# Attention followed by a gated feed-forward layer on one core: four of the twelve f chunks of the first two batches go through the pair scheme, and their weights are loaded later

## The chip, the cores and the metric

The kernel runs on one core of one Trainium2 chip. The metric is the device time of one execution in microseconds (us), as the median of several runs. TensorE is called PE below, VectorE DVE, ScalarE ACT, GpSimd POOL and SyncE SP. All loads are issued by POOL, all DMA transposes and nearly all stores by SP; an issuing instruction that has to wait holds up everything behind it on its engine.

## The reference, cut to what matters

```python
# q, k, v: (8 batches, 12 heads, 448 positions, 64)
scores = q @ k.T / sqrt(64) - log(448)
attn   = sigmoid(scores) @ v                  # per batch and head
x      = attn, heads side by side             # (8 * 448 tokens, 768)
gate   = maximum(x @ w_gate, 0)               # w_gate, w_val: (768, 1536)
val    = x @ w_val
out    = (gate * val) @ w_out                 # w_out: (1536, 768), float32
```

## The kernel before, in words

**Attention.** The work goes batch by batch. A batch has three groups `g` of four heads, and a group seven units `c` of 64 key rows. `qk_unit` (L292) does the score products of one unit (`qk`, L226, small 64x64 products) into two PSUM banks and ACT makes the sigmoids from them (L187). After a group's seven units `pv_group` (L300, L250) multiplies by `v`, and `put_xT` (L184) copies the result into `xT`, the transposed input of the feed-forward layer. The score products read `qkT`, a transposed copy of a group's k and q. For batch 0 and batch 1 PE makes it (`pe_transposes`, L195). From batch 2 on it is made by `dma_transposes` (L211): DVE copies k and q into a tile `rel` (L215), and SP issues one DMA transpose from there into `qkT` (L219). One tile of `qkT` belongs to one group; the pool has three.

**Feed-forward.** The 1536 inner columns are cut into 12 chunks `f` of 128. There are two ways to make a chunk of the gated product `hT`:

- Directly, `gv` (L304): for one batch (or for 256 or 192 of its positions, in batch 0) six products for the gate and six for the value (L309), each 128 rows deep; the maximum with zero is made on ACT (L318) or on DVE (L320), the product of gate and value on DVE (L327).
- As a pair, `gv_pair` (L510): two chunks for two batches at once with seven block products in place of eight. It needs sums of the inputs (`batch_sums_t1`, `batch_sums`, L500 to L508), a difference of the weights made in place in `wv` (`gate_sums`, L481) and sums of the weights (`unit_sums`, L485), all on DVE, and adds its partial results on ACT and DVE (L536, L540, L545).

Before the change the pair of batches 0 and 1 takes the direct way for all 12 chunks, and the three later pairs of batches take the pair way.

`down` (L341) and `down_pair` (L383) multiply `hT` by `wo` and store the output; `down_pair` needs sums of `wo` (`weight_sums`, L395).

**Order.** The schedule is written by hand, and each engine runs its instructions in the order in which the program issues them. The loop over `b` (L699) cuts the 21 units of a batch into stretches by `cuts`, and puts a few pieces of feed-forward work behind each: in batches 1 and 2, and at first in batch 3, so many direct chunks as `mix` says, taken from `gv_queue`; later one entry of `work` per stretch: a pair of chunks ("w"), a single token tile ("t") or a pair of token tiles ("y"). `hooks` run other steps within a stretch.

**Loads.** POOL issues loads in program order. The weights come in chunks with `load_gv` (L144), and `wo` with `load_o` (L162). `hold` (L653) is a tiny copy on POOL that reads a tile of `qkT`: POOL waits there until that DMA transpose has landed, and no load behind it is issued before. Tiles of k and q of batches 0, 2, 3 and later share one place; batch 1 has its own.

Of the kernel before, what the change touches and what calls it, by code (L numbers as in the profile page):

```python
# [17 lines left out]
def kernel(  # L18
# [14 lines left out]
    NPAIR = H // 2  # L33
    NG = H // 4
    P = 128
    NCH = S // 64
    NDC = DM // P
    NFC = DF // P
# [19 lines left out]
    gsbp = ctx.enter_context(tc.tile_pool(name="gsbp", bufs=6))  # L58
    first_sbuf = ExitStack()
    early = first_sbuf.enter_context(tc.tile_pool(name="early", bufs=1))  # L60
    first_psum = ExitStack()
    free = deque()

# [41 lines left out]

    def load(b, g0, g1, which, c0=0, c1=NCH):
        for nm, t16, src in zip("kq", tiles_of(b), (k, q)):
            if nm in which:
                xs, cs = slice(2 * g0, 2 * g1), slice(c0 * D, c1 * D)
                nc.gpsimd.dma_start(t16[:, xs, cs], rows_of(src, b)[:, xs, cs])  # L110

    def load_v(b):
        v16 = tiles_of(b)[2]
        nc.gpsimd.dma_start(v16[:, 0::2, :], rows_of(v, b)[:, 0::2, :])
        for r in range(2):
            nc.gpsimd.dma_start(
                v16[64 - 64 * r : P - 64 * r, 1::2, :], rows_of(v, b)[64 * r : 64 * r + 64, 1::2, :]
            )
# [25 lines left out]
    def load_gv(f0, f1, which=(0, 1)):  # L144
        fs = slice(f0 * P, f1 * P)
        for i in which:
            wt, src = ((wg, moe_w_gate), (wv, moe_w_val))[i]
            nc.gpsimd.dma_start(wt[:, :, fs], src[:, fs].rearrange("(c p) f -> p c f", p=P))
# [4 lines left out]
    load_gv(2, 4)  # L153
    load_gv(4, 6)
    load(1, 0, 1, "kq")
    load_gv(6, 9)
    load(1, 1, 2, "kq")
    load_v(1)
    load_gv(9, 12)
    load(1, 2, 3, "kq")  # L160

    def load_o():  # L162
        for m0, m1 in ((0, 512), (512, DM)):
            nc.gpsimd.dma_start(
                wo[:, :, m0:m1], moe_w_out[:, m0:m1].rearrange("(c p) m -> p c m", p=P)
            )
# [22 lines left out]

    def qkT_of(b, g):  # L190
        if (b, g) not in qkT_tiles:
            qkT_tiles[(b, g)] = qkTp.tile([P, TW, P], FP16, tag="qkT", name="qkT")
        return qkT_tiles[(b, g)]

    def pe_transposes(b, g, ti, c0=0, c1=NCH):  # L195
# [67 lines left out]
    class FirstSlot:  # L263
# [6 lines left out]
        def unit(self, u):  # L270
            qn = self.qn
            cs = range(2 * u, min(2 * u + 2, NCH))
            ps = pairp.tile([P, 2, 512], FP32, tag="pair", name="qk_ps")
            for j, c in enumerate(cs):
                qk(
                    qkT_tiles[(0, self.g)], c, self.c0, self.c1,
                    lambda hh: ps[:, hh, j * qn : (j + 1) * qn],
                )
            i = (self.number * 4 + u) % 12
            PT = early.tile([P, 2, 512], FP16, tag=f"PT{i}", name="PT")  # L280
            n = qn * len(cs)
            sigmoid(PT[:, :, 0:n], ps[:, :, 0:n])
            for j in range(len(cs)):
                self.pieces.append(PT[:, :, j * qn : (j + 1) * qn])

# [89 lines left out]
    def sub(o, a, b):  # L375
        nc.vector.tensor_tensor(out=o, in0=a, in1=b, op=AOP.subtract)
# [18 lines left out]
    def weight_sums(i):  # L395
        T = [late["T"][:, j] for j in range(4)]
        B11, B21 = wo[:, 0:HF, 0:HM], wo[:, HF:NFC, 0:HM]
        B12, B22 = wo[:, 0:HF, HM:DM], wo[:, HF:NFC, HM:DM]
        sub(T[i], *((B12, B11), (B22, T[0]), (B22, B12), (B21, T[1]))[i])
# [101 lines left out]
        T1, _, _, B11, _, B12, _ = batch_blocks(g, (0, HD))  # L501
        sub(T1, B12, B11)

    def batch_sums(g, ks):
        T1, T2, T4, _, B21, B12, B22 = batch_blocks(g, ks)
        sub(B12, B22, B12)
        sub(T2, B22, T1)
        sub(T4, B21, T2)  # L508

    def gv_pair(g, f, beside, first_copy):  # L510
        x1, x2 = xT_tiles[2 * g], xT_tiles[2 * g + 1]
# [58 lines left out]
    def push_gv(b, q0, qn, fs, act_relu=True):  # L570
        for f in fs:
            gv_queue.append(lambda f=f: gv(b, q0, qn, f, act_relu))

    def push_first(half, fs, act_relu=True):
        c0, c1 = HALVES[half]
        push_gv(0, 64 * c0, 64 * (c1 - c0), fs, act_relu)
# [57 lines left out]
            if (i, u) in after:  # L634
                after[(i, u)]()
    slots[5].pv()
    push_first(1, range(0, 6))
    for f0 in range(6, 12, 2):
        for half in range(2):
            push_first(half, range(f0, f0 + 2))  # L640


    order = [(g, c) for g in range(NG) for c in range(NCH)]
# [1 line left out]
    def pv_finish(b):  # L645
        pv_group(b, NG - 1)
        if b < 2:
            push_gv(b, 0, S, range(NFC))

    first_psum.close()  # L650
    open_banks("ring1")
# [1 line left out]
    def hold(b, g):  # L653
        nc.gpsimd.tensor_copy(gate[0:1, :], qkT_tiles[(b, g)][0:1, 0, 0:2])

    def both(b, g):
        pe_transposes(b, g, 0)
        pe_transposes(b, g, 1)

    def late_loads():  # L660
        dma_transposes(2, 2)
        hold(2, 1)
        load_o()


    work = deque()

    def push_group(g):
        tail = [("t", g, 6)] + [("y", g, p) for p in range(3)]
        if g == 0:  # L670
            tail.insert(0, tail.pop(1))
        work.extend([("w", g, f) for f in range(0, NFC, 2) if g > 0] + tail)

    def prepare():
        if work:
# [23 lines left out]
    for b in range(1, B):  # L699
        if b == 1:  # L700
            cuts, pv_at = (0, 3, 6, 9, 13, 17, 21), {3: (0, 2), 5: (1, 2)}
        elif b == 2:
            cuts, pv_at = (0, 4, 7, 11, 14, 18, 21), {0: (-1, 2), 2: (0, 2), 4: (1, 2)}
        else:
            cuts, pv_at = (0, 4, 8, 12, 16, 21), {0: (-1, 2), 2: (0, 2), 4: (1, 2)}
        count = len(cuts) - 1
        hooks = {}
        if b == 1:
            mix = (3, 3, 3, 3, 3, 2)
            hooks = {  # L710
                1: [(1, lambda: both(1, 1))],
                3: [(1, lambda: both(1, 2))],
                4: [(3, lambda: dma_transposes(2, 0))],
                5: [(2, lambda: dma_transposes(2, 1)), (0, late_loads)],
            }
        elif b == 2:
            mix = (2, 2, 1, 1, 1, 2)
            hooks = {
                2: [(0, prepare)],
                4: [(0, lambda: weight_sums(0))],  # L720
                5: [(1, lambda: weight_sums(1)), (0, lambda: weight_sums(2))],
            }
            open_late()
        elif b == 3:
            mix = (1, 1, 1, 0, 0)
        else:
            mix = (0,) * count
        for m in range(count):
            jobs = []
            for i, (g, c) in enumerate(order[cuts[m] : cuts[m + 1]]):  # L730
                if m in pv_at and i == pv_at[m][1]:
                    if m == 0:
                        pv_finish(b - 1)
                        if b == 2:
                            push_group(0)
                        elif b % 2 == 0:
                            push_group(b // 2 - 1)
                    else:
                        pv_group(b, pv_at[m][0])
                qk_unit(b, g, c)  # L740
            if m == 0 and b > 2:
                jobs.append(lambda: dma_transposes(b, 2))
            if b == 2 and m == count - 1:
                jobs.append(lambda: (dma_transposes(3, 0), dma_transposes(3, 1)))
            elif b == 3 and m == count - 1:
                jobs.append(lambda: (dma_transposes(4, 0), dma_transposes(4, 1)))
            elif 0 <= m - count + 2 and 3 < b < B - 1:
                jobs.append(lambda: dma_transposes(b + 1, m - count + 2))
            if b == 1:
                if m == 0:  # L750
                    load(2, 0, 1, "kq")
                    load(2, 1, 2, "kq")
                    load(2, 2, 3, "kq")
                    load_v(2)
            elif m == 0 and b + 1 < B:
                if b == 3:
                    jobs.append(lambda: hold(3, 2))
                jobs.append(lambda: (load(b + 1, 0, 3, "kq"), load_v(b + 1)))
            if b % 2 and b > 2:
                if m == count - 1:  # L760
                    jobs.append(lambda: (batch_sums_t1(b // 2), batch_sums(b // 2, (0, 1))))
            elif b > 3 and m == 0:
                jobs.append(lambda: batch_sums(b // 2 - 1, (1, HD)))
            if b == 2 and m == count - 1:
                ffn_mix(mix[m], hooks[m])
                next_work(jobs + [lambda: weight_sums(3)], first_act=True)
            elif mix[m]:
                for job in jobs:
                    job()
                ffn_mix(mix[m], hooks.get(m, ()))  # L770
            else:
                next_work(jobs)
            if b == 3 and m in (1, 3):
                for f in range(*((0, 8, 2), (8, NFC, 2))[m // 2]):
                    gate_sums(f, f + 2)
    pv_finish(B - 1)
    push_group(B // 2 - 1)
# [33 lines left out]
```

## Time and profile before

| | us |
|---|---|
| median of 3 runs (lowest, highest) | 396.76 (396.56, 397.04) |
| profiled execution, time | 396.35 |
| profiled execution, span of the core | 394.6 |
| PE busy | 387.5 |
| DVE busy | 279.8 |
| ACT busy | 223.2 |
| POOL busy | 49.5 |

The span runs from the first to the last instruction of the core; some 1.8 us of the execution's time lie around it. Matmuls are pipelined and the profile models their ends, so busy PE is not PE at its peak: what a product costs is seen best in the distance from one group's start to the next. The granted clock was 1.00 in every stretch.

### The profile page before, as it was taken

Reading aid. Unit: us, or ns where it says so; the run is one execution under the profiler, and the core shown is the slowest. Engines: PE = TensorE matmul, PEld = TensorE weight load, DVE = VectorE, ACT = ScalarE, POOL = GpSimd, SP = SyncE. Lnnn points to the kernel's source line nnn. Section 1 sums busy time; section 2 is a strip of 40 time slices with the busy share of each in tenths; the row PEclk is TensorE's granted clock in tenths of the full one; section 3 lists DMA queues with packets and bytes.
Section 4 is the critical chain, followed back from the end, with each engine's and each line's share of the span. In section 5 each row is a group of like instructions: output and inputs, shape, how many; then the busy total and the mean of one; then the engine's idle time right before and its main releaser. Section 6 shows DMA issues by size and latency. Waiting matters only on the chain.

```text
span 394.6 us, 8758 instructions
## 1 busy us (share of the span) xinstructions
PE 387.5 (98%) x3494; PEld 217.7 (55%) x3494; DVE 279.8 (71%) x540; ACT 223.2 (57%) x476; POOL 49.5 (13%) x73
## 2 busy tenths in 40 slices
PE   8999999999999999999999999999999999999995
PEld 3678786445455554554555545455455555555563
DVE  2453444367278899999758889999766779987663
ACT  5946778783886565655655555565566233543121
POOL 8634320500120300003000300000000000000000
PEclk9999999999999999999999999999999999999999
DMA  9999999998798891225945694223013320000135
GB/s 148 198 199 204 205 199 136 162 203 142 166 178 178 163 220 27 47 48 73 176 87 132 123 224 78 48 17 71 10 41 81 81 80 2 0 1 2 40 87 155
DMA packets 68953, 43.69 MB, mean 111 GB/s; under 512 B 35888, under 2 KB 65584, under 8 KB 68912
## 3 DMA queue, kind: packets, MB, share of 16 engines
q0 software_dynamic: 30736, 23.33, 39.5%
q1 hardware_dynamic: 37664, 19.24, 23.5%
q10 hardware_dynamic: 512, 0.56, 0.5%
q8 instruction: 27, 0.44, 0.4%
q14 instruction: 14, 0.11, 0.1%
HBM read 47.19 MB, written 11.01 MB: 147 GB/s over the span
## 4 chain that ended last, share of the span: by engine, by line
PE 91%; DMA 5%; POOL 1%; ACT 1%; issue 0%; DVE 0%; POOLq 0%; ACTq 0%
PE u L385 33%; PE g L385 16%; PE y L385 9%; PE qk_ps L232 8%; PE pv_ps L250 7%; PE g_ps L309 7%; PE v_ps L309 6%; DMA wv<-in_moe_w_val_dram 4%; PE ya L346 3%; DMA v<-in_v_dram 2%; PE yb L346 1%; PE trt L201 1%; ACT PT L187 1%; POOL k L110 1%; POOL q L110 1%
## 5 line engine op out<-in xcount | busy, mean ns | idle before, releaser
L187 ACT ACTIVATE PT<-qk_ps 128x448 f16<-128x448 f32 (+3 forms) x318 | 150.4, 595 | 70.4 <-PE qk_ps L232 70.3
L385 PEld LDWEIGHTS <-S 128*128 128x128 f16 x540 | 52.8, 98 | 43.6
L540 DVE TENSOR_TENSOR gsb<-g,gsb 128x448 f32<-128x448 f32 x72 | 42.9, 625 | 14.6 <-PE g L385 14.1
L232 PE MATMUL qk_ps<-qkT 64*64 64x448 f16 (+2 forms) x756 | 49.6, 336 | 0.8 <-DVE qkT L206 0.5
L421 ACT ACTIVATE ysb<-u 128x384 f32<-128x384 f32 x28 | 13.9, 497 | 55.5 <-PE u L385 53.4
L327 DVE TENSOR_TENSOR hT<-gate_sb,v_ps 128x256 f16<-128x256 f32 (+2 forms) x36 | 16.2, 465 | 35.5 <-ACT gate_sb L318 22.2
L536 ACT COPY gsb<-u 128x448 f32<-128x448 f32 x48 | 25.7, 566 | 23.9 <-PE u L385 22.9
L385 PEld LDWEIGHTS <-hT 128*128 128x128 f16 x294 | 28.1, 98 | 19.5 <-issue 2.1
L250 PE MATMUL pv_ps<-PT,v 64*64 64x448 f16 (+2 forms) x756 | 36.7, 329 | 0.0
L184 DVE TENSOR_SCALAR xT<-pv_ps 128x448 f16<-128x448 f32 (+2 forms) x53 | 27.9, 567 | 12.0 <-PE pv_ps L250 10.6
L309 PE MATMUL v_ps<-xT,wv 128*128 128x256 f16 (+2 forms) x216 | 33.3, 290 | 0.5 <-DMA wv<-in_moe_w_val_dram 0.4
L309 PE MATMUL g_ps<-xT,wg 128*128 128x256 f16 (+2 forms) x216 | 33.5, 291 | 0.1
L232 PEld LDWEIGHTS <-qkT 64*64 64x64 f16 x756 | 19.9, 105 | 24.7 <-issue 15.9
L385 PEld LDWEIGHTS <-wv 128*128 128x128 f16 x216 | 21.1, 98 | 19.7
L385 PEld LDWEIGHTS <-wg 128*128 128x128 f16 x216 | 20.3, 98 | 20.6 <-issue 3.0
L250 PEld LDWEIGHTS <-v 64*64 64x64 f16 x756 | 21.5, 107 | 11.1 <-issue 1.0
L385 PE MATMUL u<-T,hT 128*128 128x384 f16 x138 | 26.2, 326 | 0.0
L437 DVE SCALAR_TENSOR_TENSOR ysb<-y,ysb 128x384 f32<-128x384 f32 x24 | 13.4, 557 | 17.8 <-PE y L385 10.3
L309 PEld LDWEIGHTS <-wg 128*128 128x128 f16 x216 | 18.5, 98 | 11.5 <-issue 5.0
L110 POOL DMA_DIRECT2D k<-in_k_dram x14 | 10.9, 778 | 111.1 <-DVE rel L215 104.5
L309 PEld LDWEIGHTS <-wv 128*128 128x128 f16 x216 | 20.1, 98 | 8.4 <-DMA wv<-in_moe_w_val_dram 1.0
L385 PE MATMUL u<-xT,wg 128*128 128x448 f16 x108 | 23.5, 353 | 0.1
(69 smaller groups left out, 531.7 us busy)
## 6 DMA issues: line engine op xcount, KB each, us to landing
out_dram<-ysb SPq DMA_DIRECT2D x52, 192.0 KB, 2.9
k<-in_k_dram POOLq DMA_DIRECT2D x5, 672.0 KB, 11.7
q<-in_q_dram POOLq DMA_DIRECT2D x5, 672.0 KB, 14.6
v<-in_v_dram POOLq DMA_DIRECT2D x8, 336.0 KB, 14.7
v<-in_v_dram POOLq DMA_DIRECT2D x16, 168.0 KB, 13.9
k<-in_k_dram POOLq DMA_DIRECT2D x8, 224.0 KB, 12.0
wo<-in_moe_w_out_dram POOLq DMA_DIRECT2D x1, 1536.0 KB, 11.1
q<-in_q_dram POOLq DMA_DIRECT2D x6, 224.0 KB, 12.2
```

The costliest lines, as they stand in the source:

```text
L110: nc.gpsimd.dma_start(t16[:, xs, cs], rows_of(src, b)[:, xs, cs])
L184: nc.vector.tensor_scalar(out=xT, in0=src, scalar1=XSCALE, scalar2=None, op0=AOP.mult)
L187: nc.scalar.activation(PT_ap, ps_ap, AF.Sigmoid, bias=sig_bias, scale=qk_scale)
L232: nc.tensor.matmul(out_of(hh)[o : o + 64, :], qkT[rows, c, cols], qkT[rows, NCH + c0 : NCH + c1, cols], start=True, stop=True, tile_positi ...
L250: nc.tensor.matmul(ps[hh][64 * r : 64 * r + 64, 0:qn], v16[rows, 2 * g + hh, c * D : (c + 1) * D], pieces[c][rows, hh, :], start=(c == 0), ...
L309: nc.tensor.matmul(ps[-1][:, 0:qn], wt[:, dc, f * P : (f + 1) * P], xT_tiles[b][:, dc, q0 : q0 + qn], start=(dc == 0), stop=(dc == NDC - 1),)
L327: nc.vector.tensor_tensor(out=hT_tiles[g][:, f, o : o + qn], in0=gate_sb[:, 0:qn], in1=ps[1][:, 0:qn], op=AOP.mult,)
L346: nc.tensor.matmul(ps[:, 0 : m1 - m0], hT_tiles[g][:, f, t * P : (t + 1) * P], wo[:, f, m0:m1], start=(f == 0), stop=(f == NFC - 1),)
L385: nc.tensor.matmul(ps[:, 0:n], A[:, k_, :], W[:, k_, :], start=(first and k_ == 0), stop=(k_ == kn - 1), skip_group_check=True,)
L421: nc.scalar.activation(o, ps[:, 0:HM], AF.Copy, scale=OUT_SCALE)
L536: by(gs[u][i][:], ps[u][:, 0:S])
L540: nc.vector.tensor_tensor(out=gs[u][i][:], in0=ps[u][:, 0:S], in1=gs[u][i][:], op=AOP.add)
```

## The change

A constant `PAIR0 = 8` is added. Chunks 8 to 11 of batches 0 and 1 leave the direct queue (`push_first`, `pv_finish`) and become two pairs, the first two entries of `work`, which batch 3 runs in its first two stretches. The order after them is "t", "y", "y", "y". With them:

- Weights: chunks 8 and up are no longer loaded at the start; they are loaded in batch 2 (`late_loads`), in two pieces, between the first group and the rest of batch 3's k and q. `wo` comes last of all, behind batch 3's v.
- Batch 2: the k and q of its first group are loaded before batch 1's v; the rest of batch 2 is loaded in batch 1's second stretch, behind a new `hold(2, 0)`.
- `qkT` of batch 2's first group gets a tile of its own (`extrap`, in memory that the first slots' `PT` tiles leave), and its DMA transpose is issued in batch 1's second stretch, with no load issued behind it until it has landed. The transposes of groups 1 and 2 move to batch 2's first stretch, batch 3's first to batch 2's third stretch, batch 3's second and third to batch 3's first stretch.
- The maximum with zero of batch 0's remaining chunks goes from ACT to DVE.
- The stretches of batches 1 and 2 hold fewer direct chunks (`mix`), the sums for the new pairs are made in batch 2, and `weight_sums` moves to batch 3.

```diff
+    PAIR0 = 8
...
+    slot_sbuf = ExitStack()
+    slotp = slot_sbuf.enter_context(tc.tile_pool(name="slotp", bufs=1))
...
-    load_gv(6, 9)
+    load_gv(6, PAIR0)
     load(1, 1, 2, "kq")
+    load(2, 0, 1, "kq")
     load_v(1)
-    load_gv(9, 12)
     load(1, 2, 3, "kq")
...
-            qkT_tiles[(b, g)] = qkTp.tile([P, TW, P], FP16, tag="qkT", name="qkT")
+            pool = extrap if (b, g) == (2, 0) else qkTp
+            qkT_tiles[(b, g)] = pool.tile([P, TW, P], FP16, tag="qkT", name="qkT")
...
-    def batch_sums(g, ks):
+    def batch_sums(g, ks, which=(3, 2, 4)):
...
-    push_first(1, range(0, 6))
-    for f0 in range(6, 12, 2):
-        for half in range(2):
-            push_first(half, range(f0, f0 + 2))
+    slot_sbuf.close()
+    extrap = first_sbuf.enter_context(tc.tile_pool(name="extrap", bufs=1))
+    push_first(1, range(0, 6), False)
+    for half in range(2):
+        push_first(half, range(6, PAIR0), False)
...
-            push_gv(b, 0, S, range(NFC))
+            push_gv(b, 0, S, range(PAIR0))
...
+    def second_loads():
+        dma_transposes(2, 0)
+        hold(2, 0)
+        load(2, 1, 2, "kq")
+        load(2, 2, 3, "kq")
+        load_v(2)
+
     def late_loads():
         dma_transposes(2, 2)
         hold(2, 1)
+        load(3, 0, 1, "kq")
+        load_gv(PAIR0, PAIR0 + 2)
+        load_gv(PAIR0 + 2, NFC)
+        load(3, 1, 3, "kq")
+        load_v(3)
         load_o()
...
-        tail = [("t", g, 6)] + [("y", g, p) for p in range(3)]
-        if g == 0:
-            tail.insert(0, tail.pop(1))
-        work.extend([("w", g, f) for f in range(0, NFC, 2) if g > 0] + tail)
+        work.extend([("w", g, f) for f in range(0 if g > 0 else PAIR0, NFC, 2)])
+        work.extend([("t", g, 6)] + [("y", g, p) for p in range(3)])
...
         if b == 1:
-            mix = (3, 3, 3, 3, 3, 2)
+            mix = (2, 1, 2, 1, 2, 1)
             hooks = {
-                1: [(1, lambda: both(1, 1))],
+                1: [(1, lambda: both(1, 1)), (0, second_loads)],
                 3: [(1, lambda: both(1, 2))],
-                4: [(3, lambda: dma_transposes(2, 0))],
-                5: [(2, lambda: dma_transposes(2, 1)), (0, late_loads)],
             }
         elif b == 2:
-            mix = (2, 2, 1, 1, 1, 2)
+            mix = (2, 2, 1, 1, 1, 1)
             hooks = {
-                2: [(0, prepare)],
-                4: [(0, lambda: weight_sums(0))],
-                5: [(1, lambda: weight_sums(1)), (0, lambda: weight_sums(2))],
+                0: [(1, lambda: dma_transposes(2, 1)), (0, late_loads)],
+                2: [(1, open_late), (0, lambda: dma_transposes(3, 0))],
+                3: [(1, lambda: batch_sums_t1(0)), (0, lambda: batch_sums(0, (0, HD), (2,)))],
+                4: [(1, lambda: batch_sums(0, (0, HD), (4,))), (0, lambda: gate_sums(PAIR0, PAIR0 + 2))],
+                5: [
+                    (1, prepare),
+                    (0, lambda: (batch_sums(0, (0, HD), (3,)), gate_sums(PAIR0 + 2, NFC))),
+                ],
             }
-            open_late()
-        elif b == 3:
-            mix = (1, 1, 1, 0, 0)
...
+            if b == 3 and m == 0:
+                jobs.append(lambda: dma_transposes(3, 1))
             if m == 0 and b > 2:
                 jobs.append(lambda: dma_transposes(b, 2))
-            if b == 2 and m == count - 1:
-                jobs.append(lambda: (dma_transposes(3, 0), dma_transposes(3, 1)))
...
+            if b == 3 and m == 3:
+                jobs.append(lambda: (weight_sums(2), weight_sums(3)))
...
+            if b == 3 and m == 2:
+                weight_sums(0)
+                weight_sums(1)
```

More of the change, by code (lines that the diff above doesn't have):

```diff
@@ L279, in unit @@
             i = (self.number * 4 + u) % 12
-            PT = early.tile([P, 2, 512], FP16, tag=f"PT{i}", name="PT")
+            PT = slotp.tile([P, 2, 512], FP16, tag=f"PT{i}", name="PT")
             n = qn * len(cs)
@@ L502, in batch_sums_t1 @@
         sub(T1, B12, B11)
-    def batch_sums(g, ks):
+    def batch_sums(g, ks, which=(3, 2, 4)):
         T1, T2, T4, _, B21, B12, B22 = batch_blocks(g, ks)
-        sub(B12, B22, B12)
-        sub(T2, B22, T1)
-        sub(T4, B21, T2)
+        for i in which:
+            sub(*{3: (B12, B22, B12), 2: (T2, B22, T1), 4: (T4, B21, T2)}[i])
     def gv_pair(g, f, beside, first_copy):
@@ L740 @@
                 qk_unit(b, g, c)
+            if b == 3 and m == 0:
+                jobs.append(lambda: dma_transposes(3, 1))
             if m == 0 and b > 2:
                 jobs.append(lambda: dma_transposes(b, 2))
-            if b == 2 and m == count - 1:
-                jobs.append(lambda: (dma_transposes(3, 0), dma_transposes(3, 1)))
-            elif b == 3 and m == count - 1:
+            if b == 3 and m == count - 1:
                 jobs.append(lambda: (dma_transposes(4, 0), dma_transposes(4, 1)))
@@ L748 @@
                 jobs.append(lambda: dma_transposes(b + 1, m - count + 2))
[L749 to L755, printed above, removed]
+            if m == 0 and 2 < b < B - 1:
                 if b == 3:
@@ L763 @@
                 jobs.append(lambda: batch_sums(b // 2 - 1, (1, HD)))
[L764 to L767, printed above, removed]
+            if b == 3 and m == 3:
+                jobs.append(lambda: (weight_sums(2), weight_sums(3)))
+            if mix[m]:
                 for job in jobs:
@@ L772 @@
                 next_work(jobs)
+            if b == 3 and m == 2:
+                weight_sums(0)
+                weight_sums(1)
             if b == 3 and m in (1, 3):
-                for f in range(*((0, 8, 2), (8, NFC, 2))[m // 2]):
+                for f in range(*((0, 4, 2), (4, PAIR0, 2))[m // 2]):
                     gate_sums(f, f + 2)
```

## The prediction

> **What bounds the kernel now.** I read the page first, then PE's time by stage, then the chain in order of time, and last the DMA transposes one by one.
>
> ```profile
> PE 387.5 (98%) x3494; PEld 217.7 (55%) x3494; DVE 279.8 (71%) x540; ACT 223.2 (57%) x476; POOL 49.5 (13%) x73
> PE 91%; DMA 5%; POOL 1%; ACT 1%; issue 0%; DVE 0%; POOLq 0%; ACTq 0%
> ```
>
> PE sets the time; the 5% of DMA is the wait for the first loads, over by 28.2 us. The windows of batches 1, 2 and 3 (columns: length, then busy PE, PEld, DVE, ACT, POOL, clock, DMA share, GB/s):
>
> ```profile
> 33.50:62.40 28.90, 28.84 (x402) 22.99 (x402) 11.32 (x29) 23.34 (x60) 8.54 (x12) 1.00 1.24 194
> 62.40:99.02 36.62, 36.62 (x319) 18.66 (x319) 20.14 (x34) 24.77 (x55) 5.85 (x8) 1.00 1.06 164
> 99.02:126.73 27.71, 27.71 (x271) 14.57 (x270) 17.25 (x36) 21.37 (x48) 3.84 (x6) 1.00 0.91 171
> ```
>
> PE is never short of work here, DVE and ACT have room, and the DMA moves some 200 GB/s through batch 1. So PE work that goes is time that goes, as long as loads and transposes still come before PE asks. That is the question, since the change makes PE ask earlier.
>
> **PE work.** Chain in order of time (start, length, what): a direct chunk of 448, then one whole pair.
>
> ```profile
> 67.06 1.14 PE g_ps L309 x6
> 68.19 1.14 PE v_ps L309 x6
> ...
> 325.30 2.27 PE u L385 x12
> 327.57 1.14 PE g L385 x6
> ...
> 333.24 2.27 PE u L385 x12
> ```
>
> A direct chunk costs 2.27 us. In batch 0 a chunk is a half of 256 (two groups of 0.66) and a half of 192 (two of 0.49): 2.30. A pair runs from 325.30 to 333.24: 7.94. Removed: 4 x 2.27 + 4 x 2.30 = 18.3. Added: 2 x 7.94 = 15.9. Saved: 2.4 us. The "y" that moves from batch 2 to batch 3 costs the same there. The engines that serve PE have cover: the new sums in batch 2 are five of 1344 or 768 columns (850 or 551 ns) more, against 16 us of idle DVE; ACT has 42 sigmoids a batch, spaced 0.42 (17.8 us), against 19.7 of PE in batch 1 and 27.5 in batch 2. Without that cover, in batch 1's shortest stretches, PE would wait a few tenths for a PSUM bank: 0 to 0.5, in the next bound.
>
> **Loads in batch 1.** Eight halves (9.2 us) leave batch 1, so it ends at 62.4 - 9.2 = 53.2, and everything in it is asked for sooner. The load stream runs without a gap, so its landings shift by its bytes alone: -1.7 us for a chunk less of each weight ahead of group 1 (wv's 576 KB landed at 36.25), then +2.3 for batch 2's k and q ahead of v, and group 2's k and q no longer wait for 1152 KB of weights. Batch 1's v would be whole at 42.8 and is asked for at 42.1; group 2's q lands at 45.1 and is asked for at 44.4. Cost 0.7, up to 2.2 if the transpose of (2,0), now issued in that stream at 40, holds it up. I take 1.0. Batch 2 starts at t2 = 54.2.
>
> **The transposes.** SP's issue, then time to landing; (2,0) at 54.6 with loads behind it until 60.7, (3,2) at 102.8 alone, and (4,2), (5,2), issued together with a batch's loads:
>
> ```profile
> L219 SPq DMA_TRANSPOSE qkT<-rel x1: 3188/3188/3188, 54.6 to 54.6; - x1
> DMA to landing us min/median/max: 7.6/7.6/7.6
> ...
> L219 SPq DMA_TRANSPOSE qkT<-rel x1: 1519/1519/1519, 102.8 to 102.8; - x1
> DMA to landing us min/median/max: 4.0/4.0/4.0
> ...
> L219 SPq DMA_TRANSPOSE qkT<-rel x1: 1663/1663/1663, 131.4 to 131.4; - x1
> DMA to landing us min/median/max: 12.3/12.3/12.3
> ...
> L219 SPq DMA_TRANSPOSE qkT<-rel x1: 1587/1587/1587, 181.5 to 181.5; - x1
> DMA to landing us min/median/max: 11.5/11.5/11.5
> ```
>
> Alone 4 us; partly beside loads 7.6; wholly beside them 10.7 (at 223.0) to 12.3. Before, the long ones do no harm: they are the third groups, asked for two stretches later. The first two groups' transposes of batch 3 went at 94.9 and 96.6, after the last load (94.1).
>
> The Trainium skill says why (DMA: Bandwidth & Descriptors, "Queues, rings and completion order"): each DMA engine takes turns between its queues, packet by packet, so a transpose of many small packets waits for a load packet at each of its own. By that rule, as an estimate: in batch 1's window the load queue's 6233 packets took 111% and the transpose's 1824 took 12.4% of 16 engines for 28.9 us, 82 and 31 ns each, so its 114 turns per engine take 13 us, and the sum below would be 3 higher.
>
> Now after. The hold on (2,1) frees POOL when that transpose lands. It is issued behind batch 2's first chunk: 4.5 us of PE, 0.6 and 0.8 of DVE, 4.1 alone, t2 + 10. The first load follows 1.1 later (67.41 to 68.47 before), bytes 2 to 3 after that: t2 + 13.5. Queued there: batch 3's k, q, v (2016 KB), four weight pieces (1536 KB) and `wo` (2304 KB), together 6.0 MB, 29.4 us at the 204 GB/s of the load-only stretches. Undisturbed the stream ends at t2 + 43. Before, the last load had landed 5 us ahead of batch 3 (94.1 against 99.0); now batch 3 starts at t2 + 27.5 (stretches of 6.9, 5.3, 4.6, 3.1, 4.6, 3.1, each as long as its like before), in the middle of the stream.
>
> - (3,0): issued behind batch 2's third stretch, t2 + 18.2, asked for at t2 + 27.5. Lead 9.3 against 7.6 to 12.3: cost 0 to 3. The weight pieces land in quick small pieces; I take 0.5.
> - (3,1): in the beside part of the first pair. On DVE two copies (0.62), three sums (0.55), two copies into `rel` (0.39) come first, behind 1.14 of PE: 4.7 us after the pair's start. PE asks in the next stretch's fourth unit: 7.94 + 0.1 + three units of 0.69 together, 8.7 after the pair's start. Lead 4.0. Issued at t2 + 34.4, it has at least 8.6 us of stream beside it, all `wo`. Alone it costs 0, by the 7.6 row 3.6, by the 12.3 row 8.3. No row has `wo` beside a transpose; I take a landing of 10.0, between the rows with loads for a part and for the whole of the time: 6.0.
> - Behind the waiting unit on PE stand the second pair, "t" and all else; nothing else can run. `wo` is asked for by "t" at t2 + 49 and has landed by then if the transposes add 6 or less, and PE is 6 later itself: 0, up to 3.
> - The stop is the longest of PE's. The one stretch without matmuls before, the start, was followed by matmuls at half speed:
>
> ```profile
> 1.16 3.47 PE L175 MATMUL warm_ps<-zeros 128*128 128x448 f16 x10 [1.16 <-DVE zeros L129]
> ```
>
> Ten in 3.47 against 10 x 0.189: 1.6 us lost. Whether a stop of 6 us does that, no row shows; bounds 0 and 1.6, and as that is the only row of PE after a rest, 1.6.
>
> The skill has a rule for it (TensorE: Matmul & The Clock Gate, "Part 1: The HAM clock gate"): after an idle window of about 3.4 us the clock halves until a busy window of that length has passed. By it 1.7 would be lost, as an estimate, and nothing at a stop of 3 us, which would take 1.6 off the sum.
>
> **Sum**, against the profiled execution's 396.35: -2.4 + 1.0 + 0.5 + 6.0 + 0 + 1.6 = +6.7, 403.05. The median of the runs lies 0.4 above it: 403.5. PE has no slack later in which it could be won back.
>
> **Rivals.**
> - Faster: the transposes hold. Loads and transposes share without loss, (3,1) lands in 4 to 5 us. Then -2.4 and 0 to 1.2 from batch 1: 394.0 to 395.6 with the 0.4. For it: at 54.6 the loads beside went on at their pace, 1.1 us apart. Against: three rows of 11 us. It decides where (3,1) lands within 5.5 us of its issue. 0.19.
> - Slower by much more: the stream itself is late. Each transpose beside loads put a batch's loads back by some 5 us (131.3 to 150.1, against 13.3 alone at 107.4). Three of them, and `wo` ends at t2 + 58, where "t" asks at t2 + 49 to 52 plus the stops; the second pair's weights come late to DVE, whose queue holds the copies of `pv` behind them. Another 3 to 5: 406.5 to 408.5. 0.11.
> - No change: the stops come to 2.4 in all, as with (3,1) at 5.5 to 6.5 and none elsewhere: 396.4 to 397.2. 0.04.
>
> **Chances and range.** The forecast has 0.66 and its own range 398.5 to 407: (3,1) by 7.6 to 12.3, the clock 0 or 1.6. A difference of 0.2%, 0.8 us, is about what a measurement can tell from no change. Faster by more 0.20, within 0.04, slower 0.76. The whole range reaches into the faster rival: 395.0 to 407.5, which leaves some 0.1 below and 0.06 above.
>
> **What would show it.** In the profile after: PE stops in front of the qk products of batch 3's eighth unit, released by DMA `qkT`, for 3 to 8 us; the SP transpose before it lands over 7 us after its issue; `wo` lands after that issue; matmuls at half speed follow the stop; the window of batch 1 is 20 to 22 us long. A smaller wait at `v` or k and q in batch 1 is the 1.0. I am wrong if the transposes of batch 3 land in 4 to 5 us with loads in flight, or if PE's windows of batches 1 to 3 add up to 91 us.

## The result and the profile after

The changed kernel takes 412.96 us (median; 412.79 to 414.75) against 396.56 for the kernel before in the same session: 1.0424 times the time, 95% interval 1.0411 to 1.0437. The profiled execution took 412.79 with a span of 410.7, 16.1 more than the span before. The direction was forecast, the size was not: 403.5 was predicted, and the time lies above the range (395.0 to 407.5).

The page of the changed kernel, first its PE line and its chain by engine, then the granted clock in 40 slices:

```profile
PE 390.3 (95%) x3434; PEld 214.8 (52%) x3434; DVE 298.0 (73%) x573; ACT 220.6 (54%) x461; POOL 52.6 (13%) x78
PE 80%; DMA 11%; DVE 4%; ACT 1%; POOL 1%; issue 1%; POOLq 0%; DVEq 0%; SPq 0%; ACTq 0%
PEclk9999999979699999999999999999999999999999
```

Sixty matmuls fewer, yet PE is busy for longer: the clock dips to 7 and 6 tenths in the ninth and eleventh slices, and DMA's share of the chain rises from 5% to 11%. The windows of batch 1, of batch 2, and of batch 3 as far as its first "y" (length, then busy PE, PEld, DVE, ACT, POOL, clock, DMA share, GB/s):

```profile
33.39:53.97 20.58, 20.37 (x306) 15.18 (x306) 11.68 (x29) 18.35 (x41) 6.49 (x10) 1.00 1.05 160
53.97:81.85 27.88, 27.86 (x265) 13.57 (x264) 14.59 (x28) 22.73 (x52) 10.54 (x14) 1.00 1.04 150
81.85:126.00 44.15, 31.64 (x235) 15.28 (x235) 25.51 (x48) 17.36 (x38) 3.79 (x6) 0.85 1.11 160
```

Batch 1 was forecast at 19.7 + 1.0 and took 20.6, batch 2 at 27.5 and took 27.9. Nearly everything that went wrong is in the third row: 12.5 us in which PE did nothing, and a clock of 0.85. Batch 3 as a whole ends at 143.1, so the three batches take 109.7 us against 93.2 before. The chain in order of time shows where (start, length, what):

```profile
72.92 15.75 DMA qkT<-rel
88.67 0.04 issue
88.71 0.96 PE qk_ps L236 x8
89.67 2.61 PE pv_ps L254 x28
92.29 0.75 PE qk_ps L236 x8
93.03 1.73 PE u L389 x6
...
97.72 10.21 DMA qkT<-rel
107.93 0.04 issue
107.98 0.59 PE qk_ps L236 x4
108.56 2.35 PE u L389 x6
110.92 1.27 PE g L389 x6
```

There are two stops where one was forecast. The transpose of (3,0) is in flight for 15.75 us, and batch 3's first unit, which PE reaches at 81.85, waits for it until 88.71. The transpose of (3,1) takes 10.21, and the eighth unit waits for it. Behind each stop stand matmuls at about half their speed. SP's view of the first transpose, and for comparison of (2,1)'s, which has no load beside it (issue, then time to landing):

```profile
L223 SPq DMA_TRANSPOSE qkT<-rel x1: 4681/4681/4681, 72.9 to 72.9; - x1
DMA to landing us min/median/max: 15.7/15.7/15.7
...
L223 SPq DMA_TRANSPOSE qkT<-rel x1: 1535/1535/1535, 60.4 to 60.4; - x1
DMA to landing us min/median/max: 4.2/4.2/4.2
```

The same instruction, 4.2 us alone and 15.7 in a load stream that was already flowing when it was issued: the four late weight pieces landed at 74.8, 76.8, 80.2 and 85.5, and batch 3's other k and q at 88.4 and 90.7.

### The profile page after: what moved, and what is told of

Same layout as the page of the kernel before. It is cut to its first block, busy times and chain, and to the rows that moved or that the text cites. A ratio compares the mean times of both kernels' runs of the same rounds, so it can differ in the third digit from the quotient of the medians.

```text
span 410.7 us, 8662 instructions
## 1 busy us (share of the span) xinstructions
PE 390.3 (95%) x3434; PEld 214.8 (52%) x3434; DVE 298.0 (73%) x573; ACT 220.6 (54%) x461; POOL 52.6 (13%) x78
## 4 chain that ended last, share of the span: by engine, by line
PE 80%; DMA 11%; DVE 4%; ACT 1%; POOL 1%; issue 1%; POOLq 0%; DVEq 0%; SPq 0%; ACTq 0%
PE u L389 33%; PE g L389 16%; PE y L389 9%; PE qk_ps L236 7%; PE pv_ps L254 6%; DMA qkT<-rel 6%; DMA wv<-in_moe_w_val_dram 3%; PE g_ps L313 3%; PE v_ps L313 3%; PE ya L350 2%; DMA v<-in_v_dram 2%; ACT PT L190 1%; PE yb L350 1%; PE trt L205 1%; DVE T L380 1%
## 5 line engine op out<-in xcount | busy, mean ns | idle before, releaser
L389 PEld LDWEIGHTS <-S 128*128 128x128 f16 x576 | 56.5, 98 | 48.0 <-issue 1.5
L236 PE MATMUL qk_ps<-qkT 64*64 64x448 f16 (+2 forms) x756 | 51.5, 342 | 13.5 <-DMA qkT<-rel 12.5
L543 DVE TENSOR_TENSOR gsb<-g,gsb 128x448 f32<-128x448 f32 x80 | 47.6, 624 | 17.0 <-PE g L389 16.5
L539 ACT COPY gsb<-u 128x448 f32<-128x448 f32 x52 | 27.9, 562 | 24.0 <-PE u L389 22.9
L187 DVE TENSOR_SCALAR xT<-pv_ps 128x448 f16<-128x448 f32 (+2 forms) x53 | 27.8, 566 | 16.5 <-PE pv_ps L254 15.1
L389 PEld LDWEIGHTS <-wg 128*128 128x128 f16 x240 | 22.8, 99 | 24.4 <-issue 4.9
L389 PEld LDWEIGHTS <-wv 128*128 128x128 f16 x240 | 23.5, 98 | 21.9
L389 PE MATMUL u<-xT,wg 128*128 128x448 f16 x120 | 27.7, 369 | 0.1
L389 PE MATMUL g<-X,S 128*128 128x448 f16 x120 | 26.1, 354 | 0.0
L389 PE MATMUL g<-xT,wg 128*128 128x448 f16 x120 | 26.0, 352 | 0.0
L389 PE MATMUL u<-xT,wv 128*128 128x448 f16 x120 | 26.0, 352 | 0.0
L389 PE MATMUL g<-xT,S 128*128 128x448 f16 x120 | 26.0, 352 | 0.0
L389 PE MATMUL u<-X,S 128*128 128x448 f16 x120 | 26.0, 352 | 0.0
## 6 DMA issues: line engine op xcount, KB each, us to landing
wg<-in_moe_w_gate_dram POOLq DMA_DIRECT2D x6, 384.0 KB, 11.4
```

What stands on the lines that cost most here:

```text
L187: nc.vector.tensor_scalar(out=xT, in0=src, scalar1=XSCALE, scalar2=None, op0=AOP.mult)
L236: nc.tensor.matmul(out_of(hh)[o : o + 64, :], qkT[rows, c, cols], qkT[rows, NCH + c0 : NCH + c1, cols], start=True, stop=True, tile_positi ...
L389: nc.tensor.matmul(ps[:, 0:n], A[:, k_, :], W[:, k_, :], start=(first and k_ == 0), stop=(k_ == kn - 1), skip_group_check=True,)
L539: by(gs[u][i][:], ps[u][:, 0:S])
L543: nc.vector.tensor_tensor(out=gs[u][i][:], in0=ps[u][:, 0:S], in1=gs[u][i][:], op=AOP.add)
```

## The experiments

The theory at first (A): two transposes queued into a running stream land late, the stops halve the clock, and taking the transposes out of the stream gives the time back. The rival (B): the stream itself is late for this schedule, whoever makes `qkT`.

**1. (3,0) by PE.** `ident` gets a lasting place.

```
-   2: [(1, open_late), (0, lambda: dma_transposes(3, 0))],
-   3: [(1, lambda: batch_sums_t1(0)), ...
+   2: [(1, open_late)],
+   3: [(1, lambda: (both(3, 0), batch_sums_t1(0))), ...
```

> Group (3,0) of batch 3 is transposed by PE in batch 2's fourth stretch, the rest is as in the change (412.96). Theory A, a transpose queued into a running load stream lands late: the first stop of 6.9 us and the 2.55 us of half-speed matmuls behind it go, PE pays 0.9 for the transposes, so about 404.4; the second stop may grow by up to 2, since batch 3 then comes earlier against the same loads of wo: 404 to 407. Theory B, the load stream itself is late, whatever the transposes do: PE stops a few us later at the first pair for the weights of chunks 8 to 11, and the time stays at 409 to 413.

Measured: 411.31 (410.45 to 412.17), only 1.65 below the change. The time lies in B's range, but PE does not wait for the weights as B has it, and A had the second stop grow by 2 us at most: neither theory said this. The first stop and its half-speed matmuls are gone, but (3,1), now issued at 89.42, lands 15.1 us later:

```profile
89.42 15.13 DMA qkT<-rel
104.55 0.04 issue
104.59 0.59 PE qk_ps L236 x4
105.18 2.35 PE u L389 x6
107.53 2.24 PE g L389 x6
```

One stop of 11.1 us took the place of two of 6.8 and 5.7. Where PE comes earlier, it issues (3,1) earlier into the same stream, and waits longer. The stops are not terms that can be taken off one by one.

**2. Both groups by PE.** Also (3,1), in the middle of batch 3's second stretch.

```
+   if b == 3 and m == 1 and i == 2:
+       both(3, 1)
    qk_unit(b, g, c)
-   if b == 3 and m == 0:
-       jobs.append(lambda: dma_transposes(3, 1))
```

> Groups (3,0) and (3,1) are both transposed by PE, (3,1) in the middle of batch 3's second stretch. Theory A: both stops go (6.9 and 5.9 us), with them both times at half speed (2.55 and 1.26), and PE pays 0.9 twice: 398 to 399. What is left over the kernel before is then the two PE transposes and the late sums. Theory B: v, wo or the weights of the pairs come late in their place, 402 to 408.

Measured: 399.11 (398.69 to 399.44), ratio 1.0064 (1.0049 to 1.0079). Theory A holds for the pair of them: of 16.4 us, 13.85 were the two DMA transposes and what followed from them, net of the 1.8 that PE pays. `v`, the weights of the pairs and `wo` (landed at 103.1) make neither PE nor DVE wait. B falls.

**3. PE kept busy in the stops.**

```
+   if b == 3 and (g, c) in ((0, 0), (1, 0)):
+       warm_late(34 if g == 0 else 28)   # products nobody reads
    qk_unit(b, g, c)
```

> PE multiplies 34 times (6.4 us) ahead of batch 3's first qk unit and 28 times (5.3 us) ahead of its eighth, on data that nobody reads; the rest is as in the change. The stops end when they did. If a rest of PE is what halves the speed of the matmuls behind it, they run at full speed and the time falls by 2.55 + 1.26 = 3.8 us to about 409.2; by the single charge of the prediction it falls by 1.6, to 411.4. If the long matmuls wait for PSUM banks or late data instead, nothing falls: 413 to 414.

Measured: 414.08 (413.44 to 414.91), no gain. The cause of the long matmuls is shown all the same. The window of 4.3 us behind the first stop in the change:

```profile
88.70:93.00 4.30, 4.29 (x45) 1.86 (x46) 0.68 (x2) 2.09 (x5) 0.00 (x0) 0.50 1.25 204
```

And the window of the same place in this run:

```profile
88.50:93.00 4.50, 4.49 (x57) 2.39 (x58) 2.56 (x5) 3.97 (x9) 0.00 (x0) 1.00 1.25 204
```

The clock is 0.50 behind a rest and 1.00 behind 34 idle products; `pv` takes 1.32 in place of 2.61. But the 2.6 us won there brought (3,1)'s issue forward to 94.98, into more of the stream. It took 14.8 us, put `wo` back from 107.2 to 109.95, and the second stop ended 1.8 us later than in the change. The 28 products in front of that stop were over 4.9 us before its end, and the clock behind it was 0.50 again. As in run 1, time won in front of the second stop is lost in it.

**4. Smaller load packets.** The weights of chunks 8 to 11 one chunk at a time.

```
-   load_gv(PAIR0, PAIR0 + 2)
-   load_gv(PAIR0 + 2, NFC)
+   for f in range(PAIR0, NFC):
+       load_gv(f, f + 1)
```

> The weights of chunks 8 to 11 are loaded in eight pieces of one chunk in place of four of two: packets of half the size, twice as many, ahead of the same bytes. If a transpose takes its turns packet by packet with the loads, (3,0) lands 10 to 13 us after its issue in place of 15.75, and the first stop shrinks to 1 to 4 us. If it gets a fixed share of the DMA engines' time or bytes, it still takes 15 to 16 us and the stop stays at 6 to 7 us.

Measured, in one execution: 417.74, and 15.3 us for (3,0): the time that stood on the other side of the expectation. What follows stands behind the next run.

**5. Larger load packets.** The same weights, four chunks at a time.

```
-   load_gv(PAIR0, PAIR0 + 2)
-   load_gv(PAIR0 + 2, NFC)
+   load_gv(PAIR0, NFC)
```

> The weights of chunks 8 to 11 come in two pieces of four chunks: packets of twice the size of the change's, half as many. If each packet of the transpose takes a turn of its own length, whatever load packet goes beside it (as the run with half-size packets, 15.29 us, suggests), (3,0) again lands 15 to 16 us after its issue and more bytes of loads go through beside it, so wo lands 0 to 2 us earlier than 107.2. If a turn grows with the load packet, (3,0) takes 18 to 22 us and the first stop grows to 9 to 12.

Measured, in one execution: 412.56, and 16.9 us for (3,0), between the two expectations; `wo` landed at 104.4. Over (3,0)'s whole flight the load packets outnumber its own (3676 to 1824 in the change), but the DMA view shows that the flight has two parts. In the change, from 72.9 to 76.9, load packets move alone (queue: packets, MB, share of 16 engines):

```profile
q0 software_dynamic: 1555, 0.78, 144.1%
```

From 77.9 to 83.4 both queues move, loads first and then the transpose:

```profile
q0 software_dynamic: 1039, 0.69, 86.8%
q1 hardware_dynamic: 1034, 0.26, 45.5%
```

In the run with small packets, from 78.4 to 80.9:

```profile
q0 software_dynamic: 796, 0.20, 81.9%
q1 hardware_dynamic: 774, 0.20, 66.6%
```

And with large ones, from 77.0 to 83.0:

```profile
q0 software_dynamic: 994, 0.90, 90.6%
q1 hardware_dynamic: 995, 0.25, 31.9%
```

Once the transpose moves, one load packet goes by for each packet of its own, whatever their size: the first expectation of run 4 has the mechanism. A turn, that is one packet of each queue on one of the 16 engines, takes 52 ns beside load packets of 251 bytes on average, 85 beside 664 and 96 beside 905. Size is not all: in run 4 from 82 to 86, where small and large packets are mixed, a turn takes 106 ns beside 693 bytes. With 114 turns on each engine and 4.4 us in front of them, small packets all the way would have made some 10 us (an estimate from these rows). Run 4 took 15.3 because its expectation left out two things: no packet of the transpose moved in the first 4.4 us, and the small weight packets then lasted for half of the turns only. The rest stood beside batch 3's other k, q and v, whose packets are as large as before. With small packets the loads do worse (1.86 MB in (3,0)'s time against 2.30), and that costs too: `wo` lands at 112.0, and (3,1) takes 13.6.

**6. `wo` only behind (3,2).** `load_o()` leaves `late_loads`.

```
-   jobs.append(lambda: hold(3, 2))
+   jobs.append(lambda: (hold(3, 2), load_o()))
```

> wo is loaded only after (3,2) has landed, so (3,1) has no load beside it. (3,1) lands about 4.2 us after its issue and the second stop goes. If the transposes beside loads were the whole loss, the time falls by 5.9 + 1.3 to about 405.8. If the DMA stream up to the end of wo is what PE waits for in the end, wo lands near 119 and the direct token chunk, which asks for it near 113, stops for 5 to 8 us: 410 to 414.

Measured, in one execution: 409.78, just under the second range. (3,1) lands after 4.1 us, as alone, and the second stop is gone. SP's view of it:

```profile
L223 SPq DMA_TRANSPOSE qkT<-rel x1: 1538/1538/1538, 96.9 to 96.9; - x1
DMA to landing us min/median/max: 4.1/4.1/4.1
```

The single token chunk waits for `wo` instead (PE's waits: total, times, longest):

```profile
PE ya L350 <- DMA wo<-in_moe_w_out_dram: 2.4, 1, 2.4
PE yb L350 <- DMA wo<-in_moe_w_out_dram: 1.2, 1, 1.2
```

`wo` landed at 118.6. The wait was 3.6, less than the 5 to 8 expected: `wo` lands in two parts, and `ya` started on the first at 114.6.

**7. The transposes alone, by a hold.** Weights of chunks 10 and 11 behind batch 2's `v`; then all of batch 3's k and q, then chunks 8 and 9; (3,0) and (3,1) issued together, `v` and `wo` held until they land. Weight sums 0 and 1 early, as in run 8.

```
+   3: [..., (0, lambda: (dma_transposes(3, 0), dma_transposes(3, 1),
+                         hold(3, 1), load_v(3), load_o(), ...))],
```

> No transpose moves to PE. The weights of chunks 10 and 11 are loaded behind batch 2's v; batch 3's k and q for all groups come first behind the hold, then the weights of chunks 8 and 9; (3,0) and (3,1) are issued together behind batch 2's fourth stretch, and v and wo wait for them by a hold. First two weight sums early. Theory A, a transpose is dear only beside a running stream: (3,0) and (3,1) land 5 to 7 us after their issue, about when batch 3 starts, no stop is over 1 us and wo lands before 101: 395 to 396.5, below the kernel before. Theory B, the DMA engines have no room for all this before batch 3, wherever it is put: a stop of 3 us or more remains at batch 3's first unit or at the pairs' weights, 400 or more.

Measured: 404.99, ratio 1.0213 (1.0200 to 1.0226), some 9 above theory A. They took 6.6 and 5.8 us, as expected, and PE stopped for 1.1 us at batch 3's first unit. But k and q were whole only at 76.5, `wo` landed at 109.0 with (3,2) beside it for 16.7 us (the token chunk waited 0.9 for it), and the early weight sums waited for it on DVE: 3.4 us of PE in front of the units behind the token chunk. How much of that is the hold's and how much the sums' was not taken apart; run 8 has the sums alone.

**8. (3,1) by PE before the first pair, weight sums early.** On top of run 2.

```
+   if b == 3 and m == 0:
+       both(3, 1)                         # in place of the middle of m == 1
-   if b == 3 and m == 2:
-       weight_sums(0)
-       weight_sums(1)
-   if b == 3 and m == 3:
-       jobs.append(lambda: (weight_sums(2), weight_sums(3)))
+   if b == 3 and m in (2, 3):
+       jobs.append(lambda m=m: (weight_sums(2 * m - 4), weight_sums(2 * m - 3)))
```

> As the run with both groups on PE (399.11), with (3,1) transposed at the end of batch 3's first stretch, ahead of the first pair, and the first two weight sums put ahead of the copies of the direct token chunk. Theory A: the 1.46 us that batch 3's seventh and eighth units waited for the copies out of PSUM go, and of the waits of the first down product for its sums (0.8 and about 1) one half: 396.8 to 397.6. What is then left over the sum of PE's work is the 0.9 twice for transposes on PE. Theory B: the copies only push DVE's work later elsewhere: 398.5 to 399.5.

Measured: 401.30, 2.2 above run 2: the first half holds, the second does harm. The chain:

```profile
106.83 1.27 DVE T L380
108.10 0.02 issue
108.12 1.36 DVE T L380
...
111.61 0.61 DVE ysb L357
112.22 0.04 issue
112.26 0.71 PE qk_ps L236 x4
```

Two weight sums (`T`) of 1.3 us stand on DVE ahead of the copy `ysb` that frees a PSUM bank, and the units of PE wait 2.3 us for it. The clock has a part in the 2.2: its mean was 1.00 in two of the six executions (399.7 and 400.4) and 0.995 or 0.996 in the others (401.2 to 402.8); in the profiled one it fell to 0.50 behind this wait.

**9. Weight sums behind the second pair**, (3,1) as in run 8.

```
-   if b == 3 and m == 2:
+   if b == 3 and m == 1:
        weight_sums(0)
        weight_sums(1)
-   if b == 3 and m in (1, 3):             # gate sums of chunks 0 to 3, 4 to 7
+   if b == 3 and m in (2, 3):
```

> Both groups on PE, (3,1) at the end of batch 3's first stretch as in the run before; but the first two weight sums now stand on DVE behind the second pair, where the first gate sums stood, and these go behind the direct token chunk. So no weight sum stands ahead of the token chunk's copies. Theory A, the time left over is DVE's order there and the two PE transposes: the 2.9 us in front of the units behind the token chunk go, and the 1.46 at (3,1)'s copies stay away: 396.8 to 398.2. Theory B, the sums wait for wo (103) and push DVE's work wherever they stand: 399 to 401.

Measured: 398.84 (398.63 to 399.73), ratio 1.0066 (1.0054 to 1.0079), 0.6 above the range of theory A. PE still waits 1.3 us for that copy, now behind the token sums: in batch 3 DVE's order decides.

**10. (3,0) by DMA again, but issued early.** Batch 3's k and q of group 0 get a place of their own and are loaded behind batch 2's `v`; (3,1) by PE as in run 8.

```
+   first3 = [extrap.tile([P, 2, NCH * D], FP16, name=nm) for nm in ("k3", "q3")]
+   1: [(1, lambda: dma_transposes(3, 0))],
-   2: [(1, open_late), (0, lambda: dma_transposes(3, 0))],
+   2: [(1, open_late)],
```

> Batch 3's k and q of group 0 have a place of their own, so they are loaded right behind batch 2's v, and (3,0) is transposed by DMA again, but issued near 65, some 17 us before it is asked for, into the same running stream. (3,1) is transposed by PE at the end of batch 3's first stretch. If a transpose beside loads takes 15 to 17 us and nothing worse, it lands at 80 to 82, the first stop is 0 to 1 us, wo lands about 2 us later than with both on PE (105), and the time is 397 to 399. If the transpose is late because of where it stands in the load stream's order, and not because of its own pace, it lands after 84 again and the stop is 2 to 6 us: 400 to 405.

Measured: 399.95 (399.59 to 400.44), 0.95 above the first range. SP's view of (3,0):

```profile
L223 SPq DMA_TRANSPOSE qkT<-rel x1: 5312/5312/5312, 66.5 to 66.5; - x1
DMA to landing us min/median/max: 13.6/13.6/13.6
```

13.6 us, and no one waits: it lands at 80.2, before the 81.8 at which it is asked for. What PE pays is 1.0 us at the transposes of (3,1), whose q the stream now delivers at 85.5, and 1.3 at batch 4's first unit. Its first packet too moves 4 us after the issue, and then it goes packet for packet with the loads (1359 to 1359 from 73 to 79, 71 ns a turn beside 508 bytes). It is slow wherever it stands in the stream, and lead hides that.

**11 and 12. DVE relieved.** On top of run 9 the results in `down` are copied by ACT; in run 12 the gate sums of chunks 4 to 7 also go one stretch later.

```
-   nc.vector.tensor_scalar(out=ysb[:, m0:m1], in0=ps[:, 0 : m1 - m0], ...)
+   nc.scalar.activation(ysb[:, m0:m1], ps[:, 0 : m1 - m0], AF.Copy, scale=OUT_SCALE)
-   if b == 3 and m in (2, 3):             # run 12 alone
+   if b == 3 and m in (2, 4):
```

> As the run with both groups on PE and the first weight sums behind the second pair (398.84), but the direct token chunks' results are copied out of PSUM by ACT in place of DVE, so the units behind the first of them no longer wait for a bank that DVE frees late (1.99 us, of which 0.35 stays). Theory A, what is left is DVE's order in batch 3: 396.9 to 397.5, level with the kernel before. Theory B, DVE's work in batch 3 is the bound and the wait only moves to the down product: 398.3 to 399.

> The same, and the gate sums of chunks 4 to 7 move from the fourth to the fifth stretch of batch 3, so that the copies of the first down product's neighbour, pv, come sooner: the 0.7 us more than before in front of batch 3's last units go. Theory A: 396.2 to 396.9, level with the kernel before or 0.1% above. Theory B: DVE is late in the next batch for it: 397 to 398.

Measured: 398.03 (ratio 1.0041, 1.0026 to 1.0056) and 397.49 (1.0029, 1.0019 to 1.0038), so most of the waits went, but both ended above theory A's ranges. Run 12 lies in theory B's, though its view lists no wait of PE for DVE in the next batch. The waits that the view of PE's waits still lists in run 12, both from the start of the kernel:

```profile
PE warm_ps L178 <- DVE zeros L132: 1.2, 1, 1.2
PE qk_ps L236 <- DVE qkT L210: 0.5, 1, 0.5
```

And its chain by engine, where DMA no longer stands:

```profile
PE 93%; ACT 4%; DVE 2%; issue 0%; DVEq 0%; ACTq 0%
```

The span is 394.9 against 394.6 before: -2.4 of products, +1.8 of transposes on PE, and some 0.9 of short waits in batch 1 come to +0.3. But the profiled execution is the fastest of the ten (396.70); the medians lie 1.0 apart, and the other 0.7 stays open. No version beat the kernel before. The two PE transposes eat most of what the pairs save.

## Why the prediction was wrong

Term by term, against the span's +16.1:

| term | predicted | measured |
|---|---|---|
| PE work | -2.4 | -2.4 fits run 12 |
| batches 1 and 2 | +1.0 | +0.9 and +0.4 |
| stop for (3,0) | +0.5 | +6.9 |
| stop for (3,1) | +6.0 | +5.7 |
| `wo` late | 0 | 0 |
| clock | +1.6 | +2.6 and +1.5 |
| weight sums late on DVE | not there | +1.5 |

The measured ones add up to 17.1, 1.0 more than the span grew; each is read to some tenths.

**The step that failed** is the landing of (3,0): "Lead 9.3 against 7.6 to 12.3: cost 0 to 3. The weight pieces land in quick small pieces; I take 0.5." 12.3 was no upper end. The rows of 10.7 to 12.3 were transposes issued together with loads whose bytes come some 2 us later: (4,2) had its first packet moving after 1.2 us, and the engines to itself at first. (3,0) is the first here that is issued into a stream in full flow for all its time: its first packet moved after 4.1 us, the turns took 11.4 more, and it landed after 15.75, with a lead of 8.9. And the small pieces were no help: two of the four had landed before the first packet moved, and more than half of the turns stood beside the larger packets of k, q and v. The whole error of the sum grows from this: 6.4 us of stop and a second time at half clock.

**(3,1) was right in size by luck, and wrong in its reason.** The sum took 10.0 us of landing with the whole of `wo` still to come. Run 1 is that case, and there it took 15.1. The 10.2 came about because the first stop had put PE back by 9.5 us, and (3,1) into the last of the stream: `wo` had landed at 107.2, 0.7 us ahead of it. With (3,0) at 0.5 as forecast, the second stop would have been some 11, as in run 1, and the total hardly less: 411.3 there. Two stops that share a stream are to be costed together, as the time at which the stream lets go.

**The clock.** By the chain, 0.96 + 2.61 + 0.75 + 1.73 = 6.05 us behind the first stop against 0.50 + 1.32 + 0.38 + 1.24 = 3.44 for the same pieces in run 12: 2.6, not 1.6. Behind the second stop the first three groups take 4.05 us from start to start against 2.60 in run 2: 1.5 more. In both cases the granted clock was 0.50 for some 6.8 us (87.2 to 94.0 and 104.2 to 111.1), of which only the part behind the stop's end costs. The mechanism was right (run 3); it was charged once and from a row of ten products. The Trainium skill's rule (TensorE: Matmul & The Clock Gate, "Part 1: The HAM clock gate": half clock after an idle window of about 3.4 us) fits the first stop, where the clock fell 5.3 us after PE had stopped. It does not bound the others: at the second stop the clock fell after 2.0 us, and in run 5 a wait of 2.8 us was enough; in the 3.4 us before that fall PE had been busy for 1.3.

**The turns.** The rule of the skill from which the prediction made its estimate (DMA: Bandwidth & Descriptors, "Queues, rings and completion order": an engine takes turns between its queues, packet by packet) is what the runs show, one packet against one. The trace of before shows it too, in (4,2)'s time from 135 to 139:

```profile
q0 software_dynamic: 680, 0.60, 90.8%
q1 hardware_dynamic: 679, 0.17, 32.9%
```

The estimate of 13 us took a turn as 82 + 31 = 113 ns; measured turns are shorter than the two packets' times together, 94 ns here and 85 to 96 in the change and run 5. So its turns were some 1.5 us too long in all, and it had no start of 4 us: 13 was short of the 15.75, but nearer than the rows. The sum used it for neither group: for (3,0) it would have made the cost 3.7 in place of 0.5.

**DVE.** The sum gave the new sums cover by the idle DVE of batch 2. It did not follow the weight sums, which the change moved into batch 3: there they delay a "y" product by 0.8 and the last units by 0.7 us, and runs 8 and 9, which differ in DVE's order alone, lie 2.5 us apart, the clock behind run 8's wait included.

**The rivals.** "The transposes hold" fell: none of batch 3's first two landed under 10 us. "The stream itself is late" had the larger time but not its mechanism: in the change PE waits for neither `wo` nor the late weights, and DVE only 1.7 us for one of these, within the first stop. The lower end of "the transposes hold", 394.0, lacks the 0.4 that its upper end has. "No change" fell with the stops. The marks that were named came true: the stop at the eighth unit, 5.7 us; its transpose over 7 us; `wo` after its issue; half speed; a batch 1 of 20.6. The first unit's stop was not among them.

## What to carry to other kernels

Before moving a DMA transpose, ask what will be flowing when it is issued: here it takes 4 us alone and 13.6 to 16.9 where loads flow all the time, since its first packet moves only after some 4 us and each of its packets then waits for a load packet. Smaller load packets help only for as long as they are the ones beside it; lead hides the whole of it. Stops that hang on one stream don't add: taking one away moved PE up into the next, and 9.5 us became 1.65. A sum moved on an engine with idle time still has a place in that engine's order, and the copies that free PSUM banks stand behind it.

## What the runs showed of the hardware

A DMA transpose issued beside flowing loads moved no packet for some 4 us (3.8 to 4.4 in the change and in runs 1, 3, 4, 5, 6, 9 and 10, 2.6 to 3.1 where the loads were ending), against 1.2 alone; what holds it, the profile does not show. Then it took one turn for each load packet, and the turn grew from 52 to 96 ns as the load packets grew from 251 to 905 bytes.

In the change such a transpose cost the stream about as much as its time alone: in 15.8 us the loads moved 2.30 MB, which takes 11.3 us at the 203 GB/s that run 1 shows without a transpose (76 to 89 us); 4.5 us were lost, and alone it takes 4.0 to 4.2. About 1 us of it is a stretch from 83.6 to 84.9 in which both queues moved almost nothing (77 and 87 packets); its cause stays open. What a second transpose costs in the same stream is not shown: in run 1, (3,1) and (3,2) took 16.9 us together where (3,1) alone took 15.1, but from 101.4 on the loads were running out (288 packets to the transposes' 2186).

A rest of 1.3 us (run 9) left the clock at 1.00; one of 2.3 us (run 8) was followed by 0.50 from 113.8 to 117.1, 1.5 us after PE had started again.
